# A 7-tap convolution and a gated feed-forward block: the order of the opening's weights, loads and late passes

## The chip, the cores and the metric

One core of a Trainium2 chip runs the whole program. The metric is the device time of one execution in microseconds (us); the median of several runs stands for a kernel.

The engines in this text: PE is the matrix engine (TensorE) and PEld its weight loads, DVE is VectorE, ACT is ScalarE, POOL is GpSimd, SP is SyncE, which here only issues DMAs and waits. Each engine takes its instructions in the order in which the program gives them; semaphores carry the waits between engines.

## The reference

Input x has 8 sequences of 4096 tokens with 192 channels. Each of 8 heads has 24 channels and 7 taps; the taps are the softmax of the head's row of `weight`.

```python
w = softmax(weight)                        # 8 heads x 7 taps
y[b, s, h, :] = sum_k w[h, k] * x_pad[b, s + k, h, :]   # causal: six zero rows ahead
g = y @ w_gate                             # 192 -> 1536
v = y @ w_val
out = (g * sigmoid(g) * v) @ w_out         # 1536 -> 192
```

All inputs and the output are float32; the matrix products run in float16 with float32 sums.

## The kernel before, in words

**Blocks and chunks.** The 32768 tokens go in blocks of 512; two blocks are a pair. The 1536 hidden channels go in 12 chunks of 128. For each block and chunk, PE makes gate and val (L563 and L564, three passes of 64 rows each side by side in the two halves of the array), ACT makes silu of the gate (L568), DVE multiplies by val into `h` (L570). The second product (`acc`, L575) takes the `h` of the block before, a few pieces behind each chunk. Chunks are counted through the program: block 0 has chunks 0 to 11, block 1 has 12 to 23, pair 1 begins at 24. Gate has 2 PSUM buffers, val 3; the bank `run` is a single one, which also serves the gate of chunk 2; `acc` has one buffer of two banks.

**Convolution, normally.** From pair 1 on, each pair's x comes as squares of 32 by 32 (`sqA` for channels 0 to 127, `sqB` for the last 64 channels of both blocks; `emit_load`, L103) that DVE transposes (`emit_turn`, L114) into channels by tokens. Then three groups (0 is A's first block, 1 is B, 2 is A's second block) run the taps by channel with weights `wn`: ACT starts `run` (L490) and makes products (L483), DVE adds others onto `run` (L500), POOL makes two or three products and adds everything (L505, L512), joins the result `xc` (L518), and SP copies it with its halves swapped (`xs`, L466 and L467). SP has a wait of its own (`mark`, L460) on PE in each block.

**The opening.** Pair 0 (blocks 0 and 1) has its convolution done by PE instead, with a band matrix `T` and x as it lies in memory, because that starts earlier. Block 0: x lands in `x_sb`, is cast into `x16` by ACT and POOL, `heads` multiplies it by `T`, ACT and DVE fold the sums, `gather` sorts them by channel through `spread` into `D0`, `D1`, `D2`. `spread` is filled by four POOL copies, `place(0)` to `place(3)`. Block 1 comes later, while block 0's chunks are running: its x (`load_x(1, ...)`) is cast by POOL into `x16p` (L240, after everything else that POOL does at the start), and three late passes of `convolve` by `halves` (L366, into `acc`) follow chunks by the list `todo`: `lateA(0)`, `lateA(1)` with `outA` (ACT folds into `foldA1`, SP swaps it into `swapA1` by L674) and `lateC` (`foldC1`, `swapC1`). Chunk 12 takes the folds in its first half passes and the swaps in its second ones. In the trace these tiles stand as foldA, swapA, foldC, swapC.

**Channel taps.** `spread_taps` (L443, L444) makes `wn` for the groups: two small matmuls of `parts` (the taps in three float16 pieces, made by POOL), and a sum by DVE. Before, it stands in PE's order between the first passes of chunks 0 and 1 and their second ones.

**Order.** The schedule is by hand: instructions go to each engine as the program lists them. `at_chunk(c, f)` puts work behind chunk c (its gate, silu and h first). The plan's `opening` gives pair 1's three groups chunk numbers in the form (turn, start, ACT taps, DVE taps, POOL taps, join, swap). `loadA` issues pair 1's squares A behind the transpose of its squares B. The weights of gate and val come in three parts of four chunks (`load_w`, issued by POOL, L169), and w_out behind `x16p` (L615).

Of the kernel before, what the change touches and what calls it, by code (L numbers as in the profile page):

```python
# [14 lines left out]
    swap=(10, 11, 13),  # L15
    load=((2, -47), (3, -40), (0, -34), (1, -28)),
    opening=(
        (11, 13, (14, 15), (14, 15), 12, 16, 20),
        (2, 3, (5, 9), (4, 8), 3, 10, 13),
        (18, 20, (22, 23), (21,), 20, 23, 31),  # L20
    ),
    gate=2, val=3, lead=4, third=(2,),
# [4 lines left out]
def kernel(  # L27
# [9 lines left out]
    nc = tc.nc  # L37
    fp32 = mybir.dt.float32
# [10 lines left out]
    P = 128  # L49
# [3 lines left out]
    TB = P * SUBS  # L53
    NCH = Dff // P
# [21 lines left out]
    squares, xts = {}, {}  # L76
# [5 lines left out]
    def emit_load(q, part, half=None):  # L82
        head = q % ppb == 0
        if part == 2 and not half:
            squares[q, "A"] = headA if head else xpool.tile(
                [P, HIST + 2 * TB], fp32, tag="sqA", name="sqA"
            )
            squares[q, "B"] = headB if head else xpool.tile(
                [P, HIST + TB], fp32, tag="sqB", name="sqB"
            )  # L90
        for k in range(2):
            quad = 2 * (part % 2) + k
            if part < 2:
                tile_, t0, n, c = squares[q, "A"], 0, 2 * TB, SQ * quad
            else:
                tile_, t0, n, c = squares[q, "B"], TB * (part % 2), TB, P + SQ * k
            skip = HIST if head and t0 == 0 else 0
            row = q * 2 * TB + t0 - HIST + skip
            n = n // SQ + 1 - skip // SQ
            if half is not None:  # L100
                first = TB // SQ + 1
                skip, row, n = ((skip, row, first), (first * SQ, row + first * SQ, n - first))[half]
            nc.sync.dma_start(  # L103
                out=tile_[quad * SQ : (quad + 1) * SQ, skip : skip + n * SQ].rearrange("p (n c) -> p n c", c=SQ),
                in_=x_flat[row : row + n * SQ, c : c + SQ].rearrange("(n p) c -> p n c", p=SQ),
            )
# [9 lines left out]
    def sync_after(ins, earlier, why="one bank, two halves of the array"):  # L116
        tc.add_manual_dep(
            ins.ins,
            earlier.ins.name,
            mybir.DependencyInfo(mybir.DependencyClass.Sync, mybir.DependencyReason.DATA),  # L120
            reason=why,
        )
# [4 lines left out]
    HALF, STEP, W, NW = TB // 2, 85, 96, 6  # L127
# [20 lines left out]
    def load_x(b, lo, hi, queue=nc.sync):  # L148
        queue.dma_start(
            out=x_sb[0:LOADED, b, lo:hi, :],  # L150
            in_=bass.AP(
                tensor=x_flat.tensor,
                offset=x_flat.offset + (b * TB + starts[b][lo]) * D,
                ap=[[D, LOADED], [STEP * D, hi - lo], [1, D]],
            ),
        )
# [10 lines left out]
    def load_w(lo, hi, which):  # L167
        rows, src = w_halves[which]
        nc.gpsimd.dma_start(out=w[rows, :, lo * P : hi * P], in_=src[:, :, lo * P : hi * P])  # L169
# [52 lines left out]
    nc.vector.memset(spread, 0.0)  # L222

    mask = const_pool.tile([RT, D], fp16, tag="mask", name="mask")
    load_w(0, 4, 0)
    load_w(0, 4, 1)


    x16 = xpool.tile([P, NW, D + 8], fp16, tag="x16", name="x16", bufs=1)
# [47 lines left out]
    def repeated(t):  # L277
        return t[:, :].unsqueeze(1).to_broadcast([RT, REP, 8])
# [4 lines left out]
    left_second = nc.vector.scalar_tensor_tensor(  # L283
        out=left[0:RT, 1, :, :], in0=repeated(turned), scalar=norm, in1=left[0:RT, 0, :, :],
        op0=ALU.mult, op1=ALU.subtract,
    )
    left = left[:, :, :, :].rearrange("r i n m -> r i (n m)")

    sync_after(nc.sync.nop(), left_second, "squares behind the first weights")
    if n_pairs > 1:  # L290
        for part in (2, 3):
            emit_load(1, part, None)
    load_x(1, 0, 3)
    load_x(1, 3, NW)
    nc.scalar.activation(two, one, AF.Silu)
    cast(nc.scalar.copy, 0, 3)
    sync_after(cast(nc.gpsimd.tensor_copy, 3, NW), left_second, "not beside the taps")
# [1 line left out]
    def place(k):  # L299
        lo, hi, at = ((0, DB, 0), (DB, 96, 0), (0, 32, 32), (32, 96, 0))[k]  # L300
        nc.gpsimd.tensor_copy(
            spread[:, k, :, at : at + hi - lo], plain[:, lo:hi].unsqueeze(1).to_broadcast([P, 2, hi - lo])
        )

    place(0)
    place(1)
    nc.gpsimd.memset(mask, 0.0)
    nc.gpsimd.affine_select(
        out=mask[:, :].rearrange("r (h c) -> r h c", h=H),
# [1 line left out]
        pattern=[[-8, H], [0, grp]],  # L311
        compare_op=ALU.not_equal, fill=1.0, base=0, channel_multiplier=1,
    )
    load_w(4, 8, 0)
    load_w(4, 8, 1)
    place(2)
    place(3)
    own = const_pool.tile([RT, P], fp16, tag="own", name="own")
    nc.gpsimd.tensor_copy(
        own[:, :].rearrange("h (t c) -> h t c", t=2),  # L320
# [7 lines left out]
    nc.gpsimd.tensor_tensor(rest, raw, parts[:, 0, :], op=ALU.subtract)  # L328
    nc.gpsimd.tensor_copy(parts[:, 1, :], rest)
    nc.gpsimd.tensor_tensor(parts[:, 2, :], rest, parts[:, 1, :], op=ALU.subtract)  # L330
    for b in range(2):
        load_w(8, NCH, b)

# [20 lines left out]
    def convolve(banks, quarters, parts, parities):  # L356


        fresh = set()
        for part in parts:  # L360
            for e in parities:
                for n in range(len(quarters[0])):
                    for a, q in enumerate(quarters):
                        x, h, u0, out = q[n](e)
                        k = len(banks) * out.start // TB
                        ins = nc.tensor.matmul(  # L366
                            banks[k][32 * a : 32 * a + 32, out], x,
                            T[0:ROWS, part, h, u0 : u0 + out.stop - out.start],
                            start=part + e == 0 and (a, k) not in fresh,
                            stop=part == 1 and e == parities[-1], skip_group_check=True,  # L370
                        )
                        fresh.add((a, k))
        return ins
# [10 lines left out]
    def by_block(b, half):  # L384
        def of(e, w):
            h = 32 * b // grp
            h += (h + e) % 2
            return x16p[0:ROWS, e, w, 32 * b : 32 * b + 32], h, *piece(1, w, HALF * half)

        return [lambda e, w=w: of(e, w) for w in range(half * NW // 2, (half + 1) * NW // 2)]  # L390
# [49 lines left out]
    def spread_taps(bank):  # L440
        ps = bank[:, 0 : 6 * K].rearrange("p (g t k) -> p g t k", g=2, k=K)
        for g, which in enumerate((mask[:, 0:P], own)):
            nc.tensor.matmul(ps[:, g, :, :], which, parts, start=True, stop=True)  # L443
        nc.vector.tensor_reduce(wn, ps.rearrange("p g t k -> p g k t"), axis=AX.X, op=ALU.add)  # L444
# [180 lines left out]
    tpool = ctx.enter_context(tc.tile_pool(name="run", bufs=1, reuse_waits="tile", space=bass.MemoryType.PSUM))  # L625
# [6 lines left out]
    def at_chunk(c, f):  # L632
        todo.setdefault(c, []).append(f)
# [27 lines left out]
    def late_sum():  # L661
        late["sum"] = apool.tile([P, 2, 512], fp32, tag="acc", name="acc")

    def halves(g, bank):
        return convolve([bank], [by_block(2 * g + a % 2, a // 2) for a in range(4)], (0, 1), (0, 1))

    def lateA(g):
        if g == 0:
            late_sum()
        halves(g, late["sum"][:, g, :])  # L670

    def exchange(out, fold):
# [18 lines left out]
        at_chunk(2 * NCH, blank)  # L691

    late = {}
    at_chunk(5, lambda: lateA(0))
    at_chunk(6, lambda: lateA(1))
    at_chunk(6, outA)
    at_chunk(8, lateC)

    def loadA(half):
        if not half:  # L700
# [4 lines left out]
    if n_pairs > 1:  # L705
        for g, plan in enumerate(PLAN["opening"]):
            plan_group(1, g, *plan)
        for half, c in enumerate((2, 16)):
            at_chunk(c, lambda half=half: loadA(half))
    for q in range(2, n_pairs):  # L710
        base = 2 * NCH * q
        for part, c in PLAN["load"]:
            c = {2: 20, 3: 20, 0: 26, 1: 27}[part] if q == 2 else base + c
            at_chunk(c, lambda q=q, part=part: emit_load(q, part))
        for g in range(3):
            c = base + PLAN["start"][g]
# [13 lines left out]
    for n in range(2 * n_pairs):  # L730
        block = Block(n)
        for j in range(NCH):
            src, units = before if j < NCH - lead // 4 else block, late_start.get(at, 4)
            if n == 0:
                src, units = block, 0
            elif n == 2 * n_pairs - 1 and src is block:
                units = 0
            los, his = src.second(units)
            half = src.done // (2 * NCH) - 1 if units and src.done % (2 * NCH) == 0 else None
            if n == 0 and j < 2:  # L740
                if j == 0:
                    block.first(0, (0,))
                    block.first(1, (0,))
                    spread_taps(tpool.tile([P, TB], fp32, tag="run", name="run"))
                block.first(j, (1, 2))
            elif half is None:
                block.first(j)
            for lo, hi in zip(los, his):
                lo()
                hi()  # L750
            if half is not None:
                src.evacuate(half)
                block.first(j)
            block.gate(j)
            if half is not None:
                src.store(half)
            for f in todo.pop(at, ()):
                f()
            at += 1
        before = block  # L760
# [61 lines left out]
```

## Time and profile before

| what | value |
|---|---|
| median of 3 runs | 773.06 us (772.67 to 773.37) |
| the profiled execution | 773.51 us, of which span 771.7 us |
| PE busy | 763.0 us, 99% of the span |
| POOL, ACT, DVE busy | 668.7, 661.5, 658.4 us |
| granted clock of PE | 1.000 |
| block 1's x: issue, and landing of its second half | 6.76 and 7.30; 14.86 us |
| chunks 4 to 7's weights: issues | 6.36 and 7.01 us |
| swapA: issue and landing | 18.76; 23.50 us |

The profile comes from one execution; its times count from the span's start. Some 1.8 us of an execution lie outside the span. In the windows a row has the stretch, its length, then the busy time of PE, PEld, DVE, ACT and POOL with counts of instructions, the granted clock, the DMA engines' share and GB/s. In the chain of waits a row has start, length and what the time went to; "SPq" is an issue by SP, "DMA a<-b" a transfer. Queue q0 carries POOL's transfers, q1 SP's.

### The profile page before, as it was taken

The page shows a single profiled execution, that of the slowest core. Times are in us where ns is not written, and L with a number is a line of the kernel's source. Part 1 is how long each engine was busy: PE and PEld are TensorE (multiplying, and loading weights), DVE is VectorE, ACT ScalarE, POOL GpSimd, SP SyncE. Part 2 cuts the span into 40 slices and gives each one's busy share as a digit, 9 for nine tenths or more (in the row PEclk, how much of TensorE's full clock was granted, in tenths as well). Part 3 has the DMA queues.
Part 4 walks back from the last instruction along what each step waited for, and adds up shares of the span by engine and source line. Part 5 has one row for each costly group of instructions (what it writes and reads, how often), then busy time and mean ns, then how long its engine had stood idle before and what let it go on. Part 6 is the DMA issues. An engine that isn't in the chain of part 4 may idle for free.

```text
span 771.7 us, 28287 instructions
## 1 busy us (share of the span) xinstructions
PE 763.0 (99%) x11036; PEld 596.0 (77%) x11036; DVE 658.4 (85%) x1046; ACT 661.5 (86%) x1188; POOL 668.7 (87%) x654
## 2 busy tenths in 40 slices
PE   7999999999999999999999999999999999999998
PEld 3767777777777777777777777777777777778997
DVE  6788888889888888888888888888888888888875
ACT  6788888888888888888888888888888888888875
POOL 6898988888988889988889888899888899888850
PEclk9999999999999999999999999999999999999999
DMA  8553344433444343444334434334343433443211
GB/s 143 101 109 83 83 95 85 93 87 79 88 88 93 85 85 87 87 88 96 83 80 86 94 84 95 86 83 87 82 99 82 89 85 87 89 89 90 62 46 54
DMA packets 255287, 67.28 MB, mean 87 GB/s; under 512 B 207920, under 2 KB 255152, under 8 KB 255152
## 3 DMA queue, kind: packets, MB, share of 16 engines
q1 hardware_dynamic: 252048, 63.48, 37.6%
q0 software_dynamic: 2800, 1.77, 1.7%
q8 instruction: 86, 1.41, 0.8%
q14 instruction: 49, 0.40, 0.2%
q10 hardware_dynamic: 304, 0.22, 0.1%
HBM read 29.65 MB, written 25.17 MB: 71 GB/s over the span
## 4 chain that ended last, share of the span: by engine, by line
PE 96%; DMA 2%; SPq 1%; DVE 0%; ACT 0%; issue 0%; POOL 0%; DVEq 0%
PE val L564 48%; PE acc L575 34%; PE gate L563 13%; DMA x_sb<-in_x_dram 1%; DMA swapA<-foldA 1%; SPq L103 0%; DMA sqB<-in_x_dram 0%; PE acc L773 0%; PE idle L257 0%; POOL x16p L240 0%; PE val L773 0%; PE run L773 0%; DVE h L570 0%; ACT foldA L677 0%; SPq L467 0%
## 5 line engine op out<-in xcount | busy, mean ns | idle before, releaser
L570 DVE TENSOR_TENSOR h<-silu,val 128x512 f16<-128x512 f16 x768 | 508.9, 680 | 102.2 <-ACT silu L568 70.3
L568 ACT ACTIVATE silu<-gate 128x512 f16<-128x512 f32 x768 | 453.1, 594 | 81.2 <-PE gate L563 72.7
L575 PE MATMUL acc<-wo_sb,h 64*128 64x192 f16 x6048 | 465.6, 243 | 1.1 <-DVE h L570 1.1
L512 POOL TENSOR_TENSOR t<-t,t 128x512 f32<-128x512 f32 x310 | 393.9, 1271 | 61.1 <-ACT t L483 37.9
L575 PEld LDWEIGHTS <-h 64*128 64x128 f16 x6048 | 394.9, 94 | 60.8 <-DVE h L570 1.4
L563 PE MATMUL gate<-xc,w_sb 64*128 64x512 f16 x1116 | 409.8, 376 | 0.0
L564 PE MATMUL val<-xc,w_sb 64*128 64x512 f16 x1116 | 409.7, 376 | 0.0
L563 PE MATMUL gate<-xs,w_sb 64*128 64x512 f16 x1116 | 360.1, 376 | 0.0
L564 PE MATMUL val<-xs,w_sb 64*128 64x512 f16 x1116 | 360.0, 376 | 0.0
L564 PEld LDWEIGHTS <-w_sb 64*128 64x128 f16 x2340 | 211.8, 94 | 96.8 <-issue 1.8
L563 PEld LDWEIGHTS <-w_sb 64*128 64x128 f16 x2340 | 212.0, 94 | 5.0 <-issue 1.5
L518 POOL TENSOR_TENSOR xc<-t,aD 128x512 f16<-128x512 f32 x93 | 118.1, 1270 | 7.3
L505 POOL TENSOR_SCALAR t<-xtA,wn 128x512 f32<-128x512 f32 x155 | 106.1, 696 | 0.7 <-DVE xtA L114 0.7
L483 ACT ACTIVATE t<-xtA,wn 128x512 f32<-128x512 f32 x124 | 88.6, 714 | 0.0
L613 ACT COPY o<-acc 128x384 f32<-128x384 f32 x126 | 60.4, 479 | 18.7 <-PE acc L575 5.4
L500 DVE SCALAR_TENSOR_TENSOR aD<-xtA,wn,run 128x512 f32<-128x512 f32 x62 | 45.9, 740 | 0.0
L483 ACT ACTIVATE t<-xtB,wn 128x512 f32<-128x512 f32 x62 | 44.3, 714 | 0.0
L490 ACT ACTIVATE run<-xtA,wn 128x512 f32<-128x512 f32 x62 | 42.5, 686 | 0.6 <-DVE xtA L114 0.6
L505 POOL TENSOR_SCALAR t<-xtB,wn 128x512 f32<-128x512 f32 x62 | 42.3, 697 | 0.0
L114 DVE STREAM_TRANSPOSE xtA<-sqA 128x544 f32<-128x544 f32 (+1 forms) x48 | 34.6, 721 | 1.0 <-DMA sqA<-in_x_dram 1.0
L500 DVE SCALAR_TENSOR_TENSOR run<-xtB,wn,run 128x512 f32<-128x512 f32 x31 | 23.2, 749 | 0.0
L500 DVE SCALAR_TENSOR_TENSOR run<-xtA,wn,run 128x512 f32<-128x512 f32 x31 | 23.2, 749 | 0.0
(112 smaller groups left out, 178.9 us busy)
## 6 DMA issues: line engine op xcount, KB each, us to landing
out_dram<-o SPq DMA_DIRECT2D x127, 192.0 KB, 2.0
sqA<-in_x_dram SPq DMA_DIRECT2D x92, 132.0 KB, 3.1
xs<-xc SPq DMA_DIRECT2D x186, 64.0 KB, 2.0
sqB<-in_x_dram SPq DMA_DIRECT2D x96, 68.0 KB, 2.3
headA<-in_x_dram SPq DMA_DIRECT2D x28, 128.0 KB, 2.7
headB<-in_x_dram SPq DMA_DIRECT2D x14, 68.0 KB, 2.5
headB<-in_x_dram SPq DMA_DIRECT2D x14, 64.0 KB, 2.1
x_sb<-in_x_dram SPq DMA_DIRECT2D x3, 216.0 KB, 5.0
```

What stands on the lines that cost most here:

```text
L483: mul(parts[-1], *self.tap(k))
L490: nc.scalar.mul(self.aD, *self.tap(0))
L500: nc.vector.scalar_tensor_tensor(out=self.aD, in0=v, scalar=s, in1=run, op0=ALU.mult, op1=ALU.add)
L505: self.product(k, lambda t, v, s: nc.gpsimd.tensor_scalar(t, v, scalar1=s, scalar2=1.0, op0=ALU.mult, op1=ALU.mult), self.parts)
L512: nc.gpsimd.tensor_tensor(self.parts[0], self.parts[0], t, op=ALU.add)
L518: nc.gpsimd.tensor_tensor(xc, self.parts[0], self.aD, op=ALU.add)
L563: nc.tensor.matmul(g, w[0:DB, ca, f], a[0:DB, :], start=(i == 0), stop=(i == 2))
L564: nc.tensor.matmul(v, w[DB:P, cb, f], b[DB:P, :], start=(i == 0), stop=(i == 2))
L568: nc.scalar.activation(s, self.g.pop(j), AF.Silu)
L570: nc.vector.tensor_tensor(h, s, self.v.pop(j), op=ALU.mult)
L575: ins = nc.tensor.matmul(acc, self.h[j][r, ts(s, P)], wo_r[r, j, :], start=first and j == 0, stop=not first and j == NCH - 1, skip_group_c ...
L613: nc.scalar.copy(self.o[:, 2 * half : 2 * half + 2, :], self.acc[:, :, 0:D])
```

## The change

Five things are moved; the arithmetic stays.

- POOL issues the weights of chunks 4 to 7 directly behind those of chunks 0 to 3, and those of chunks 8 to 11 behind the four `place` copies; mask, `own` and `parts` come after these issues.
- SP issues block 1's x ahead of pair 1's squares B.
- `spread_taps` runs behind chunk 1, in the second bank of `acc`.
- The late passes run behind chunks 4, 5 and 7, where they ran behind 5, 6 and 8.
- In the plan of pair 1, group 0 has its transpose at chunk 12 (11 before) and POOL's taps at 13 (12). Group 1 has its transpose at 3 (2), its start and POOL taps at 4 (3), ACT taps at 6 and 9 (5 and 9), DVE taps at 5 and 8 (4 and 8). The first half of squares A is issued at chunk 3 (2).

```diff
     opening=(
-        (11, 13, (14, 15), (14, 15), 12, 16, 20),
-        (2, 3, (5, 9), (4, 8), 3, 10, 13),
+        (12, 13, (14, 15), (14, 15), 13, 16, 20),
+        (3, 4, (6, 9), (5, 8), 4, 10, 13),
         (18, 20, (22, 23), (21,), 20, 23, 31),
...
-    load_w(0, 4, 0)
-    load_w(0, 4, 1)
+    for lo in (0, 4):
+        for b in range(2):
+            load_w(lo, lo + 4, b)
...
-    sync_after(nc.sync.nop(), left_second, "squares behind the first weights")
+    sync_after(nc.sync.nop(), left_second, "block 1's x behind the first weights")
+    load_x(1, 0, 3)
+    load_x(1, 3, NW)
     if n_pairs > 1:
         for part in (2, 3):
             emit_load(1, part, None)
-    load_x(1, 0, 3)
-    load_x(1, 3, NW)
...
     place(0)
     place(1)
+    place(2)
+    place(3)
+    for b in range(2):
+        load_w(8, NCH, b)
     nc.gpsimd.memset(mask, 0.0)
...
-    load_w(4, 8, 0)
-    load_w(4, 8, 1)
-    place(2)
-    place(3)
...
-    for b in range(2):
-        load_w(8, NCH, b)
...
+    def late_taps():
+        late_sum()
+        spread_taps(late["sum"][:, 1, :])
+
     def lateA(g):
-        if g == 0:
-            late_sum()
         halves(g, late["sum"][:, g, :])
...
-    at_chunk(5, lambda: lateA(0))
-    at_chunk(6, lambda: lateA(1))
-    at_chunk(6, outA)
-    at_chunk(8, lateC)
+    at_chunk(1, late_taps)
+    at_chunk(4, lambda: lateA(0))
+    at_chunk(5, lambda: lateA(1))
+    at_chunk(5, outA)
+    at_chunk(7, lateC)
...
-        for half, c in enumerate((2, 16)):
+        for half, c in enumerate((3, 16)):
             at_chunk(c, lambda half=half: loadA(half))
...
                     block.first(1, (0,))
-                    spread_taps(tpool.tile([P, TB], fp32, tag="run", name="run"))
                 block.first(j, (1, 2))
```

## The prediction

> **What bounds the kernel now.** I read the page's chain of waits first, then busy time by stage, then the chain in order of time.
>
> ```profile
> PE 96%; DMA 2%; SPq 1%; DVE 0%; ACT 0%; issue 0%; POOL 0%; DVEq 0%
> ```
>
> TensorE carries 96% of the span, and nothing in its steady work changes. So a gain can only be TensorE idle time of the opening. Stages (length, then busy time of PE, PEld, DVE, ACT, POOL):
>
> ```profile
> 14.00:17.50 3.50, 1.70 (x63) 0.81 (x65) 1.96 (x4) 1.85 (x4) 2.56 (x4) 1.00 0.57 90
> 22.00:24.00 2.00, 1.30 (x15) 0.64 (x12) 1.59 (x4) 1.05 (x3) 1.71 (x2) 1.00 0.33 80
> 24.00:37.00 13.00, 13.00 (x257) 12.39 (x256) 10.27 (x16) 10.97 (x20) 11.77 (x12) 1.00 0.43 88
> 37.00:39.00 2.00, 0.86 (x16) 0.43 (x12) 1.50 (x3) 1.43 (x4) 1.84 (x3) 1.00 0.20 62
> ```
>
> The second column is PE: full from 24 to 37, with holes before 24 and another near 38. The chain (start, length, what) names both. First hole:
>
> ```profile
> 7.30 7.56 DMA x_sb<-in_x_dram
> 14.91 1.28 POOL x16p L240 x2
> ...
> 18.15 0.59 ACT foldA L677
> 18.76 4.74 DMA swapA<-foldA
> 23.54 0.27 PE gate L563
> ```
>
> Block 1's x lands at 14.86, is cast, convolved late, folded, swapped by DMA, and block 1's first chunk (chunk 12) can only use the swap at 23.54. Second hole:
>
> ```profile
> 32.10 0.47 SPq L466
> ...
> 34.98 2.40 DMA sqB<-in_x_dram
> ...
> 38.17 0.66 DVE h L570
> 38.88 0.26 PE acc L575 x2
> ```
>
> SP issues A0's swap (group A, first half, of pair 1) at 32.10, behind it the squares B of pair 2; they land at 37.38, and VectorE stands at their transpose. So I work out one instant, T, when chunk 12 takes its swapped operands (23.54 before), and then what the second hole does.
>
> **Front, to chunk 4.** GpSimd's issues of chunks 4 to 7 (0.65 + 0.63) move from 6.36 to 3.58. It idled from 3.58 to 4.68, so its x cast starts at 2.09 + 0.85 + 0.64 + 0.65 + 0.63 = 4.86, call it 4.88: 0.20 late. The heads' second half is not touched: it waited until 6.37 for T anyway. foldA and D0 come 0.2 late (D0 ends 8.28). The spreads 2 and 3 no longer stand behind DMA issues, so the last gathers start at 7.70 (foldC's 7.61 plus a hop) and not 7.93; D1 is cast by 8.82, D2 by 8.94. The taps no longer stand in front of chunk 0's second pass, which waited until 9.62 for `parts`; it starts at 8.90. Gain so far 0.72.
>
> The taps now come after chunk 1, at 9.77 on PE. GpSimd's parts: cast 4.88, 0.61 to the spreads, four at 0.20, issues 1.27, mask 0.67, own 0.26, parts 1.25: 9.75. So PE loses about 0.1. Their bank is D1's, read out by 8.82, and the second late pass, which takes it next, comes long after the reduce. The reduce of wn (0.20) now sits between h1 and h2 on VectorE; chunks 3 and 4 wait for val buffers from h0 and h1, ahead of it. Chunk 3 starts at 10.90 (11.65 before). Chunk 4 waited for weights until 12.66; with them issued 2.8 earlier it starts at 11.55, and h3 ends at 12.85. The issues now run beside VectorE's tap operations (3.40 to 4.61), where before GpSimd stood still; no row shows the two together. I take nothing: the issues took 0.63 to 0.66 wherever they stood. If they cost the taps 0.3 of their 1.2 us, that is hidden up to the 0.95 found below.
>
> **Transfers.** Service goes in bursts. Per stretch (queue: packets, MB, share), 9.5 to 10.25, 10.5 to 11.25, and 17.5 to 21.5:
>
> ```profile
> q1 hardware_dynamic: 242, 0.18, 79.9%
> q0 software_dynamic: 54, 0.04, 35.5%
> ```
>
> ```profile
> q0 software_dynamic: 115, 0.12, 93.6%
> q1 hardware_dynamic: 62, 0.04, 25.9%
> ```
>
> ```profile
> q0 software_dynamic: 1312, 0.50, 117.1%
> ```
>
> x and weights take turns by whole transfers, and swapA, issued at 18.76, moves nothing before 21.5, while w_out's 576 KB run. The engines are full from 6 to 14, so times add up. From 6.25, where chunks 0 to 3's weights end: weights of 4 to 7 2.0 (384 KB at the 190 GB/s of the stretch 12.5 to 14), x 1.7 (432 KB, bursts at 240 GB/s or a little over), squares B 1.6 (272 KB; 119 GB/s while SP was issuing them, 200 to 217 in the best slices), weights of 8 to 11 2.0. x's data end at 9.5 to 10.2. Landing comes later than the bulk: 0.4 for squares B, 2.3 for x's second half. So x lands between 10.3 and 12.2; I take 11.4.
>
> The Trainium skill, page "DMA: Bandwidth & Descriptors", section "Queues, rings and completion order", says that each engine alternates between queue rows after at most 64 descriptors; the 17.5 to 21.5 row does not show that for swapA. By that rule swapA would land about 1.5 sooner and the sum would be set by ScalarE (below), with nothing else moved.
>
> **Block 1's x and the late passes.** The passes are the same, one chunk earlier each. The casts follow landing, the first late pass ends 1.84 after it (14.86 to 16.70 before): 13.24, and chunk 5 follows. This is covered as long as x lands by 12.8, since another wait is later:
>
> **Squares B behind x.** They now issue at 5.65 to 7.73, behind x, among the weights of 8 to 11. In order of arrival their data end at 6.25 + 2.0 + 1.7 + 1.6 + 1.0 = 12.55, taking turns at 13.55; with a landing lag of 0.4 to 2.0 the ends are 12.9 and 15.6. I take 13.8: the means of the two orders (13.05) and a lag nearer to the squares' own row. The transpose is placed one chunk later, yet VectorE reaches it at 12.85. So it stands for about 0.95 us, with h4 behind it, and ScalarE's `run` behind the transpose:
>
> ```profile
> 12.71 0.73 DVE L114 STREAM_TRANSPOSE xtB<-sqB 128x544 f32<-128x544 f32 x1
> ...
> 13.54 0.69 ACT L490 ACTIVATE run<-xtB,wn 128x512 f32<-128x512 f32 x1 [0.65 <-DVE xtB L114]
> ```
>
> `run` starts 0.83 after the transpose and holds ScalarE 0.63; silu 5 therefore starts at 13.8 + 0.05 + 0.83 + 0.63 = 15.3. From there ScalarE is continuous: silu 5 0.50, foldA 0.58, silu 6 0.49, tap 0.61, silu 7 0.50, foldC 0.36, silu 8 and 9 0.99, tap 0.61, silu 10 0.59, in all 5.23. Chunk 12 needs silu 10's gate buffer: 20.6 with a hop, and its swap pass follows 0.35 later: T = 20.95. TensorE's own passes fit below it.
>
> **The swap.** loadA's four DMAs follow the transpose on SP (1.92), so swapA issues at 16.6 and 17.2, foldA ending at 16.4. It has 3.8 us to land after the second issue; 4.5 was the case beside w_out, 1.9 to 2.6 for other swaps. w_out is issued at 12.7, not 16.13, so its data end near 18.6, plus 0 to 1.5 for the squares A now beside it; swapA lands 1.5 after (23.5 against 22.0): 20.1 to 21.6. SwapC issues from 18.4 and needs until about 21.2, its place 0.33 behind T. I keep T = 20.95: 2.6 earlier than 23.54.
>
> **The second hole.** A0's transpose moves from chunk 11 to 12: behind h12, which waits for T. Counted in before's times, h12 ends at 25.45, the transpose at 26.15, and GpSimd's group A0, which began at 24.80, begins there: 1.35 later relative to TensorE. Its work is continuous, 6.76 (24.80 to 31.56), so xc ends at 32.91 and SP's swap goes from 32.10 to 32.95. Squares B of pair 2, the transpose and h23 follow: the second hole grows by 0.85. SP had 0.5 us of slack there; it is used up. The 0.3 us that ScalarE's later `run` takes from chunk 16 vanishes in the same hole.
>
> **Sum:** 2.6 - 0.85 = 1.75 us. The profiled execution was 773.51 (771.7 span plus 1.8 around it) and becomes 771.75; against the median 773.06, 771.3. A measurement here can tell about 0.2%, 1.55 us.
>
> **Rivals.**
> - *Squares land with the third weights' middle* (14.1 to 15.5): everything from the transpose slips one for one, T is 21.25 to 22.65, the gain 0 to 1.5: 771.6 to 773.1, no change by the bound. For it: x's second half landed 2.3 after its bulk. Against it: squares landed 0.4 after theirs. 0.38.
> - *Slower: squares land only after the last weights.* Decides at 23.54 - 0.85 = 22.69 for T, so at a landing of 15.55; the last weights' DMA needed 6.0 from its issue at 10.15, and behind a backlog of 7.3 us, not 5.5, a lag of 2.7 puts the squares at 16.3: T = 23.45, 0.75 lost, 773.8; slower by over 1.55 needs 17.1. The same section of the Trainium skill says that a completion signal lands only after every earlier write of that engine, on all its queues; x's second half agrees (6 packets of its queue after 12.5, landing at 14.86), no row here shows it for squares. 0.12, of which 0.07 lies over the bound, with the mishaps not named here.
> - *Everything covered:* squares land by 12.85; silu 5 starts at 14.3, T = 20.0, gain 2.7: 770.4. If A0's group also finds its slack, 769.5. 0.1.
> - *The reorder does nothing for x*: it lands with the weights at 14 or later. Then chunk 5 is 1.2 later than ScalarE's path and T about 22.1; 772.5. The 9.5 to 10.25 row speaks against it. 0.02, counted within 0.2%.
>
> **How the numbers follow.** The forecast case (landing 13 to 14.1) has 0.38, with 770.5 to 771.6; 771.3 is its time. Faster by over 0.2% is this and the covered case, 0.48; within 0.2% the first and the last rival and the milder half of the slower one, 0.45; slower 0.07. The range 770.3 to 773.5 leaves out about 0.05 below and 0.12 above; it takes in the ends 12.9 and 15.6 of the squares' landing.
>
> **What would show it.** Right: the chain of the opening no longer holds x_sb; chunk 0's second pass at 8.9; chunk 4 without a weights wait; the wait list has the transpose of xtB on squares B, near 1 us; chunk 12's swap pass near 21; the wait on squares B of pair 2 longer than 1.3 us, h23 about 1.75 earlier. Wrong: VectorE passes the first transpose without a wait; x16p still first in PE's waits; swapA landing past 22; or SP's swap of A0 still held by TensorE rather than by GpSimd.

## The result, and the profile after

The changed kernel takes 774.93 us (median of 16 runs, 773.18 to 776.99); the kernel before took 773.07 us beside it (16 runs). The ratio is 1.0022, 95% interval 1.0012 to 1.0033: slower; the interval reaches from under to over the 0.2% that a measurement here can tell. The forecast was 771.3, range 770.3 to 773.5. The profiled execution took 775.58 us, its span is 773.8 (before: 773.51 and 771.7).

**The share of the chain and the stages.** The chain of the profile's page, then busy time by stage (start and end, length, PE, PEld, DVE, ACT, POOL, granted clock, DMA share, GB/s):

```profile
PE 95%; DMA 1%; SPq 1%; POOL 1%; issue 1%; DVE 1%; ACT 0%; DVEq 0%; POOLq 0%; ACTq 0%
```

```profile
14.00:17.50 3.50, 2.90 (x108) 1.56 (x109) 1.32 (x2) 0.69 (x2) 2.24 (x3) 1.00 0.55 62
22.00:24.00 2.00, 1.36 (x12) 0.50 (x8) 2.00 (x4) 1.16 (x3) 1.59 (x2) 1.00 0.38 76
24.00:37.00 13.00, 12.34 (x243) 11.85 (x244) 9.91 (x17) 9.73 (x18) 10.38 (x11) 1.00 0.34 70
37.00:39.00 2.00, 1.97 (x28) 1.10 (x22) 0.47 (x1) 1.94 (x4) 1.84 (x3) 1.00 0.86 178
37.00:41.00 4.00, 1.97 (x28) 1.10 (x22) 1.80 (x4) 2.49 (x5) 3.76 (x4) 1.00 0.49 106
```

PE (third number) gained 1.2 us between 14 and 17.5, because block 1's x comes earlier. It lost 0.66 between 24 and 37, where it was full before, and stands still from 39 to 41.

**The first hole.** The chain in order of time (start, length, what):

```profile
9.28 6.67 DMA sqB<-in_x_dram
15.95 0.02 issue
15.97 0.76 DVE xtB L114
...
16.81 0.69 ACT run L489
17.50 0.52 ACT silu L567
...
22.56 0.60 ACT silu L567
23.17 0.18 SPq L675
23.34 0.04 issue
23.39 1.87 DMA swapC<-foldC
...
25.30 0.28 PE val L563
```

The late x is gone from the chain, as forecast. In its place stand pair 1's squares B (landed 15.95), behind them VectorE's transpose, ScalarE's `run` and its row of silus, and at the end swapC, landed at 25.26. On PE, chunk 12's first pass, its first pass with swapped operands (the forecast's T) and its first one with the last swap are:

```profile
22.72 0.27 PE L562 MATMUL gate<-foldA,w_sb 64*128 64x256 f16 x1 [0.27 <-ACT silu L567]
...
23.62 0.27 PE L562 MATMUL gate<-swapA,w_sb 64*128 64x256 f16 x1 [0.25 <-DMA swapA<-foldA]
...
25.30 0.27 PE L563 MATMUL val<-swapC,w_sb 64*128 64x256 f16 x1 [0.38 <-DMA swapC<-foldC]
```

ScalarE's silu of chunk 10 lets chunk 12 begin at 22.72, where the forecast had 20.6. T is 23.62: forecast 20.95, before 23.54. The passes behind T then wait once more for swapA (24.21) and for swapC (25.30). The wait list from 12 to 42 us (engine, line, releaser: total, times, longest):

```profile
DVE xtB L114 <- DMA sqB<-in_x_dram: 5.1, 2, 2.9
ACT run L489 <- DVE xtB L114: 5.0, 2, 3.5
POOL x16p L241 <- DMA x_sb<-in_x_dram: 3.5, 1, 3.5
```

Before, the same list has for this wait only the one on pair 2's squares B:

```profile
DVE xtB L114 <- DMA sqB<-in_x_dram: 1.3, 1, 1.3
```

The forecast had about 1 us in the first row's longest wait; it is 2.9, and the same row holds the wait on pair 2's squares B, 2.2 (5.1 less 2.9).

**The second hole,** from the same chain:

```profile
26.31 0.76 DVE xtA L114
...
27.15 1.37 POOL t L504 x2
...
32.63 1.28 POOL xc L517
33.93 0.47 SPq L465
...
36.81 2.73 DMA sqB<-in_x_dram
...
40.34 0.66 DVE h L569
```

A0's transpose stands behind h of chunk 12 (25.68 to 26.3), GpSimd's A0 directly behind it, SP's swap directly behind GpSimd (33.93), and pair 2's squares B land at 39.54. h23 starts at 40.34, 2.17 later than before.

**Two numbers hold the whole difference.** h of chunk 12 starts at 25.68 instead of 24.80: 0.88 later, where the forecast had 22.2 (T of 20.95, and 1.26 from T to h12 as before). From there to the span's end it is 748.1 instead of 746.9: 1.2 more, forecast 0.85. Together 2.1, the difference of the spans. I call them *h12* and *the distance*, and read each experiment by them. But h12 moves from one execution to the next: e7 below, whose program is the same up to there, has 24.38 in its profile, 1.3 earlier. One profile's h12 shows no difference smaller than that.

### The profile page after: what moved, and what is told of

It reads as the page before. It is cut to its first block, busy times and chain, and to the rows that moved or that the text cites. A ratio compares the mean times of both kernels' runs of the same rounds, so it can differ in the third digit from the quotient of the medians.

```text
span 773.8 us, 28288 instructions
## 1 busy us (share of the span) xinstructions
PE 763.7 (99%) x11036; PEld 525.3 (68%) x11036; DVE 658.0 (85%) x1046; ACT 658.2 (85%) x1188; POOL 667.8 (86%) x654
## 4 chain that ended last, share of the span: by engine, by line
PE 95%; DMA 1%; SPq 1%; POOL 1%; issue 1%; DVE 1%; ACT 0%; DVEq 0%; POOLq 0%; ACTq 0%
PE gate L562 56%; PE acc L574 32%; PE val L563 6%; DMA sqB<-in_x_dram 1%; SPq L103 1%; POOL t L511 0%; PE acc L774 0%; DMA swapC<-foldC 0%; PE idle L258 0%; ACT silu L567 0%; DVE h L569 0%; POOL t L504 0%; POOL xc L517 0%; PE val L774 0%; PE run L774 0%
## 5 line engine op out<-in xcount | busy, mean ns | idle before, releaser
L574 PEld LDWEIGHTS <-h 64*128 64x128 f16 x6048 | 290.1, 94 | 127.6 <-DVE h L569 2.3
L574 PE MATMUL acc<-wo_sb,h 64*128 64x192 f16 x6048 | 363.1, 243 | 2.1 <-DVE h L569 2.1
L489 ACT ACTIVATE run<-xtB,wn 128x512 f32<-128x512 f32 x31 | 21.3, 687 | 5.0 <-DVE xtB L114 5.0
```

The lines of the kernel that those rows point to most:

```text
L489: nc.scalar.mul(self.aD, *self.tap(0))
L574: ins = nc.tensor.matmul(acc, self.h[j][r, ts(s, P)], wo_r[r, j, :], start=first and j == 0, stop=not first and j == NCH - 1, skip_group_c ...
```

## The experiments

Line numbers in the edits' text are the changed kernel's. Times are medians; the ratio is to the kernel before on the same chip, with its 95% interval.

### Where did the squares stay? The order of the weights, the order on SP

`e1_squares_first`: SP's order of before, all else changed.

```diff
-    load_x(1, 0, 3); load_x(1, 3, NW)
     for part in (2, 3):
         emit_load(1, part, None)
+    load_x(1, 0, 3); load_x(1, 3, NW)
```

> The changed kernel with SP's order of before: squares B ahead of block 1's x. Theory SQUARES (the loss is VectorE and ScalarE standing at the first transpose until squares B land at 15.95, because they are queued behind x on SP): squares land near 9 to 10, the transpose runs near 12.9 without a wait, block 1's x lands at 14 to 15, chunk 12 takes its swaps near 23, and the time is 772.5 to 773.5. Theory WEIGHTS (the loss is that chunks 4 to 7's weights, issued early, keep the engines from everything else): squares still land after 12.9 and x after 15, and the time stays at 774.5 to 775.5.

Measured 777.71, ratio 1.0060 (1.0047 to 1.0073). Issued first, at 4.64, the squares still landed only at 15.1. From their issues to landing, here and before, where they were issued at the same time:

```profile
DMA to landing us min/median/max: 7.1/7.9/8.4
```

```profile
DMA to landing us min/median/max: 2.7/2.8/2.9
```

So it is not x ahead of them that holds them. Both signs of WEIGHTS came (squares after 12.9, x after 15), but the time is 2.2 us over its range, because of something no theory had: x landed at 16.16, PE had nothing to do, and the granted clock (third number from the right) was cut.

```profile
14.00:16.00 2.00, 0.00 (x0) 0.00 (x0) 0.88 (x2) 0.04 (x1) 0.00 (x0) 0.71 0.18 47
16.00:18.00 2.00, 0.86 (x40) 0.67 (x44) 0.44 (x1) 0.66 (x1) 1.78 (x3) 0.50 0.40 63
18.00:20.00 2.00, 2.00 (x50) 0.77 (x42) 0.00 (x0) 0.19 (x1) 1.88 (x3) 0.50 0.87 98
```

`e2_weights_back`: GpSimd's order of before, x still ahead of the squares.

```diff
-    for lo in (0, 4): ...               # weights of chunks 0 to 7 first
+    load_w(0, 4, 0); load_w(0, 4, 1)    # 4 to 7 behind the mask, 8 to 11 behind parts
```

> The changed kernel with GpSimd's order of before (chunks 4 to 7's weights at 6.4, chunks 8 to 11's behind the taps' parts); x stays ahead of squares B. Theory WEIGHTS: x lands near 8.5 to 9.5, squares B near 11 to 12, ahead of the transpose; chunk 4 waits for its weights until about 13; chunk 12 takes its swaps near 21.5, and the time is 771 to 772.5. Theory SQUARES (behind x is what counts): squares still land near 14 or later, and the time is 774 to 775.

Measured 773.43, ratio 1.0006 (0.9997 to 1.0014): no loss against the kernel before can be told. This lies between the two theories: the time is 0.9 us over the range of WEIGHTS and 0.6 under that of SQUARES, squares B landed at 13.97, as SQUARES had it, and VectorE still waited 0.9 for them; h12 came at 23.77. The DMA queues between 6 and 8 us (queue: packets, MB, share of the 16 engines; q0 carries GpSimd's weights, q1 SP's x and squares) show what differs. Before:

```profile
q1 hardware_dynamic: 2062, 0.26, 82.6%
q0 software_dynamic: 54, 0.04, 17.6%
```

The changed kernel:

```profile
q0 software_dynamic: 189, 0.17, 78.2%
q1 hardware_dynamic: 9, 0.01, 1.4%
```

With the weights back:

```profile
q1 hardware_dynamic: 950, 0.46, 91.0%
q0 software_dynamic: 50, 0.04, 12.5%
```

With chunks 4 to 7's weights queued at 3.58, SP's queue moved 9 packets in these two microseconds, although x had been issued at 4.64; the two queues together moved 0.18 MB, where it is 0.30 before and 0.50 in e2. The 16 engines were busy for only 80% of this time, so whether x stood there for want of an engine, or because its own descriptors came late, the trace does not show. Nor does any run separate the two parts that e2 puts back: chunks 8 to 11's weights too were early in the changed kernel (issued at 6.24, before at 9.50). The picture repeats: in the ten profiles with the weights early and x first (the changed kernel and nine variants below), q1 moved 9 to 74 packets between 6 and 8, q0 0.17 to 0.27 MB; in the five with the weights back, q1 moved 950 to 1115 packets. Squares B landed at 15.6 to 17.0 wherever the first group shows it, at 13.6 to 14.7 in the second. SP itself is held as well. The DMA issues of SP (start, length, what), changed kernel:

```profile
4.64 0.82 SPq L149 DMA_DIRECT2D x_sb<-in_x_dram  x2
5.50 6.03 SPq L103 DMA_DIRECT2D sqB<-in_x_dram  x4
16.81 2.70 SPq L103 DMA_DIRECT2D sqA<-in_x_dram  x4
19.61 3.10 SPq L675 DMA_DIRECT2D swapA<-foldA  x2
```

Four issues of squares B took 6.03 us; in e2 they took 2.73, before 2.08:

```profile
4.64 2.08 SPq L103 DMA_DIRECT2D sqB<-in_x_dram  x4
```

### The front alone

`e4_taps_only`: the kernel before with the channel taps behind chunk 1.

```diff
+    at_chunk(1, late_taps)
...
-                    spread_taps(tpool.tile([P, TB], fp32, tag="run", name="run"))
```

> The kernel before with one part of the change: the channel taps behind chunk 1, in the accumulator's second bank. Chunk 0's second pass starts near 9.2 and not at 9.62, but the first late pass still waits for block 1's x at 14.9. All theories: no change, 772.8 to 773.4; if the reduce between h1 and h2 cost something, it would be 773.3 to 773.8.

Measured 772.78, ratio 1.0003 (0.9994 to 1.0013), no change, as expected. Chunk 0's second pass starts at 9.11 (9.62 before), so the front does gain. h12 came at 24.06 and not at 24.80, but because x landed at 14.1 in this profile and at 14.86 in the one before; that transfer is not part of the edit, and what the front gains does not reach the time.

### The second hole

`e5_group0_back`: the changed kernel with group A0's plan of before.

```diff
-        (12, 13, (14, 15), (14, 15), 13, 16, 20),
+        (11, 13, (14, 15), (14, 15), 12, 16, 20),
```

> The changed kernel with group 0's plan of before: A0's transpose at chunk 11 and GpSimd's taps at 12. Theory SECOND HOLE (0.85 us of the loss comes from A0's transpose standing behind h12, which starts GpSimd's group A0 late and SP's swap and pair 2's squares B after it): GpSimd starts A0 right behind its join of B near 24.9 and not at 27.15, SP's swap of A0 is again released by TensorE near 33.2, and the time falls by 0.7 to 0.9, to about 774.1. Rival (the second hole has another cause, the first hole alone made the loss): no change, 774.6 to 775.2.

Measured 774.26, ratio 1.0017 (1.0008 to 1.0026). GpSimd starts A0 at 24.75, right behind group B, SP's swap goes at 31.91, the wait on pair 2's squares B falls from 2.2 to 1.3, and the distance from 748.1 to 747.25. With the transpose at chunk 12 it is 747.8 to 748.05 in e1, e2, e3, e7, f1 and f2; with the plan of before it is 746.6 to 746.9 in the kernel before, e4, f4 and g4. The remaining profiles with it at chunk 12 lose more behind h12 for other reasons (squares A in e6, the clock in e8, group B in f3, w_out in g1 and h1). So the trace bears the second-hole step out; the time is as expected, but its interval overlaps that of the changed kernel, so that it shows no fall by itself.

`e7_pair2_squares_early`: the changed kernel with pair 2's squares B issued behind chunk 17 (20 before), so that they do not follow A0's swap on SP.

```diff
-            c = {2: 20, 3: 20, 0: 26, 1: 27}[part] if q == 2 else base + c
+            c = {2: 17, 3: 17, 0: 26, 1: 27}[part] if q == 2 else base + c
```

> The changed kernel with pair 2's squares B issued behind chunk 17 and not behind chunk 20, so that on SP they stand ahead of A0's swap. Theory SECOND HOLE: VectorE no longer waits for them at 37.5 (2.2 us in the changed kernel's trace), TensorE's hole near 39 closes, and the time falls by about 2, to 772.7 to 773.1. Rival (the hole follows GpSimd's lag, and something else of pair 1's groups stops the chain as late): a fall of under 0.7, to 774.2 or more.

Measured 774.89, ratio 1.0020 (1.0009 to 1.0030): nothing gained. The wait of VectorE on these squares is gone, and with it PE's hole at 36 to 40, but in the stretch from 28 to 48 VectorE now waits for squares A of group A2, and PE for SP's `mark`, which queues behind the squares' issues:

```profile
DVE xtA L114 <- DMA sqA<-in_x_dram: 1.6, 1, 1.6
...
PE acc L574 <- SPq L459: 1.1, 1, 1.1
```

### VectorE's stand, and the swaps behind it

`f1_group1_late`: group B three chunks later, so that nobody stands for squares B.

```diff
-        (3, 4, (6, 9), (5, 8), 4, 10, 13),
+        (6, 7, (9, 11), (8, 10), 7, 11, 13),
...
-        for half, c in enumerate((3, 16)):
+        for half, c in enumerate((6, 16)):
```

> The changed kernel with group B of pair 1 moved back by three chunks: its transpose behind chunk 6, start and GpSimd taps behind 7, ScalarE taps 9 and 11, VectorE taps 8 and 10, join 11, squares A behind chunk 6. STANDING theory (what was lost is the 2.93 us that VectorE stood for squares B, and ScalarE behind it): squares B have landed when VectorE comes to them, no wait over 0.3 there, ScalarE has no 3.48 us wait, h12 of chunk 12 starts near 22.0 instead of 25.68, and with 747.9 to 748.1 from there the span is 770.0 and the time 771.8 (771.3 to 772.6). SWAPS rival (the standing only covered the transfers of the swaps behind w_out): no wait at the squares, but swapA and swapC still land at 23.5 or later and h12 starts at 24.0 or later: 773.8 or more. CLOCK rival: TensorE's hole before the late passes (x lands at 13.25) is followed by a granted clock under 0.9 and the time is 775 or more.

Measured 774.55, ratio 1.0016 (1.0004 to 1.0028). VectorE no longer waits at the first transpose, and h12 came at 24.75, 0.9 earlier than in the changed kernel's profile, but not earlier than in those of e5 and e7 (24.45, 24.38), where VectorE stands as in the changed kernel. The swaps rival holds: SP now issues squares A from 18.80 to 21.57 and swapC behind them, and PE waits for swapC until 23.8. What the stand costs by itself is not shown: without it, the swap is as late.

`e3_squaresA_late`: squares A behind the swaps on SP (`enumerate((8, 16))`). `e6_weights_back_squaresA_late`: the same on top of e2.

> The changed kernel with the first half of squares A issued behind chunk 8 and not behind chunk 3, so that SP issues both swaps ahead of it. Theory SWAPS (chunk 12 took its swaps at 25.3 because SP was still issuing squares A and their queue stood behind w_out): swapA is issued at 18.5, swapC at 20.4, they land by 22.5, chunk 12 takes them near 23, and the time is 772.5 to 773.3. Theory SQUARES (ScalarE's chain behind the late transpose sets chunk 12 at 22.7 and the rest is small): 774 to 774.7.

> e2 (GpSimd's order of before, x ahead of squares B) with the first half of squares A behind chunk 8. Theory SWAPS (once x is early, chunk 12 waits only for swaps that stand behind squares A, which stand behind w_out on SP's queue): swapA is issued near 16.7 and lands by 20, chunk 12 takes its swaps near 21.3 (about 23 in e2), and the time is 771.2 to 772. Rival (squares A come too late for A0's transpose, and VectorE stands there): the first hole closes but the second grows by as much, 773 to 774.

e3: 777.33, ratio 1.0052 (1.0039 to 1.0065). The swaps were in time, but squares B landed at 16.7 in this profile, ScalarE stood 4.4 us, PE waited 1.8 for it, and then ran at half clock:

```profile
18.00:20.00 2.00, 1.17 (x30) 0.58 (x33) 1.24 (x3) 2.00 (x5) 1.92 (x3) 0.87 1.49 181
20.00:22.00 2.00, 2.00 (x48) 1.04 (x38) 1.45 (x3) 1.12 (x3) 1.58 (x2) 0.50 0.43 78
```

e6: 775.01, ratio 1.0023 (1.0012 to 1.0034). SwapC was issued at 18.38 instead of 20.9, but squares A landed only at 24.86, A0's transpose waited 1.79 for them and GpSimd 2.7 behind it. The rival's mechanism holds, though the time is 1 us over its range: the swap's gain is paid by the squares moved behind it.

`f2_w_out_split`: w_out in two DMAs, the second half issued behind chunk 8. `g1_w_out_half_behind_11`: behind chunk 11. `h1_w_out_half_behind_h9`: when h of chunk 9 is done.

```diff
-    nc.gpsimd.dma_start(out=wo_r, in_=...)
+    load_wo(0, NCH // 2)
...
+    at_chunk(8, lambda: load_wo(NCH // 2, NCH))    # f2; 11 in g1; a wait on h9 in h1
```

> The changed kernel with w_out in two DMAs, the second half issued behind chunk 8. SWAPS theory (squares A and the swaps stand in line behind w_out's data): swapA's second issue is no longer held until 22.7, swapC lands by 23.5 instead of 25.26, ScalarE's silu 10 then sets chunk 12, h12 starts near 24.0 instead of 25.68: span 772.0, time 773.8 (773.3 to 774.3). STANDING rival: ScalarE's path, late by the squares' landing, sets chunk 12 anyway; h12 moves by less than 0.5, time 774.5 to 775.

> The changed kernel with w_out in two DMAs, the second half issued behind chunk 11 (in f2_w_out_split it was issued at 19.38, 0.3 us ahead of the swaps' first issue at 19.71). SWAPS theory (the swaps wait for whatever data were queued before them): with only 288 KB of w_out, issued near 13.7, and squares A in front, swapA lands by 22.5, swapC by 23.3, and h12 starts near 23.8 (ScalarE's path) instead of 25.68: span 771.9, time 773.7 (773.2 to 774.3). Rival: squares A alone, or the swaps' own two issues, hold them; swapC lands past 24.5 as in f2, h12 after 25.0, time 774.8 or more.

> The changed kernel with w_out in two DMAs; GpSimd issues the second half only when h of chunk 9 is done (near 22.2), behind the swaps' issues and some 5 us ahead of the place where g1's TensorE stood for it (27). SWAPS theory: as in g1 both swaps land about 2 us after their issue, h12 starts near 24.9 (25.68 before the edit), no wait on w_out over 0.5: span 772.9, time 774.1 to 774.8. Rival: the half lands after 27.5, TensorE stands for it and time is 775.5 or more.

f2: 775.62, ratio 1.0028 (1.0018 to 1.0038). The half was issued at 19.38, just ahead of swapA (19.71), and swapA took 3.5 to 4.3 us to land: no gain, h12 at 25.79. g1: 777.88, ratio 1.0062 (1.0050 to 1.0074). With the half behind them the swaps land in 1.8 to 2.0 us. SwapA, then swapC, from issue to landing:

```profile
DMA to landing us min/median/max: 1.9/2.0/2.0
```

```profile
DMA to landing us min/median/max: 1.8/1.8/1.9
```

SwapA took 2.1 to 4.0 us in the changed kernel and 3.5 to 4.3 in f2, and here SP's second issue of it was not held either. So the swaps do wait for the data of w_out queued ahead of them. h12 came at 24.95, 0.73 earlier than in the changed kernel's profile, but later than in e7's with w_out whole, so that this difference is no price. And the half, issued at 25.48, is needed from 27 on. PE stands for it:

```profile
PE acc L574 <- DMA wo_sb<-in_moe_w_out_dram: 3.2, 1, 3.2
```

h1: 777.14, ratio 1.0043 (1.0030 to 1.0055). The swaps land in 1.8 to 2.0 again, the half goes out only at 24.21, where 22.2 was expected, because squares B landed at 17.0 in this profile, and PE stands 1.9 us for it. Here the rivals hold: of the three places tried for the half, one is ahead of the swaps and two are too late.

`f3_group1_late_w_out_split` joins f1 and f2. `f4_before_w_out_split` and `g4_before_w_out_half_behind_8` are e4 with w_out split, the half behind chunk 4 or 8.

> Both edits together. If each cost lies on its own path and the later one sets chunk 12, both removed give h12 near 21.8, span 769.9, time 771.7 (771.0 to 772.4), and less than either alone by at least 0.5. If the rivals hold (granted clock cut after the hole at 13 to 14, or squares A late for A0's transpose, whose landing then sets group A0), 774 or more.

> The kernel before with the channel taps behind chunk 1 and w_out in two DMAs, the second half issued behind chunk 4. The late x stays (landing near 14). SWAPS theory: swapA lands near 21 instead of 22.7, h12 starts 1 us or so earlier than with the taps alone (24.06), span 769.9, time 771.7 (771.2 to 772.3). Rival: the second half of w_out is now the one that stands in front of the swaps, or is late for block 0's second product behind chunk 15; no gain, 772.8 or more.

> The kernel before with the channel taps behind chunk 1 and w_out in two DMAs, the second half issued behind chunk 8, where GpSimd waits 0.9 us anyway (in f4 it was issued at 18.92, ahead of the swaps at 19.33). SWAPS theory: swapA (issue 17.98) lands near 21 instead of 22.74, h12 starts near 23.0 instead of 24.06: span 769.9, time 771.7 (771.2 to 772.3). Rival: the second half runs into swapC (issue 19.74), or TensorE's hole at 14 to 16 is followed by a cut clock as in f4 (0.50 from 16 to 18): 773.5 or more.

f3: 774.37, ratio 1.0022 (1.0010 to 1.0034); h12 at 23.05, 2.6 earlier than in the changed kernel's profile and 1.3 earlier than in e7's, but the distance is 748.5: group B ends later on GpSimd, and A0 starts only behind it, at 25.47. f4: 774.08, ratio 1.0019 (1.0007 to 1.0030), swapA landed at 23.9, since its data now follow the second half, issued at 18.92. g4: 774.35, ratio 1.0022 (1.0012 to 1.0032), where I expected that half behind the swaps; GpSimd reached it at 19.3, ahead of swapA at 19.76. All three miss the times forecast, f4 and g4 because the half still lay ahead.

### The clock

`e8_filled_hole`: five products of zeros behind chunk 4 of the changed kernel, into a bank not yet in use, so that PE stands less there.

> The changed kernel with five matmuls of zeros behind chunk 4, into the accumulator's bank that the first late pass then overwrites; they stand where TensorE waited from 12.8 to 14.0. Theory CLOCK (part of the loss, and the spread of the changed kernel's times from 773.2 to 777.0, is the clock being cut in runs in which TensorE's holes before chunk 12 grow long; the mean clock of its runs was between 0.996 and 1.0): the clock stays at 1.000 in nearly all runs, the median falls to 774.2 to 774.7 and the spread shrinks to 1.5 us. Rival (the spread comes from the DMA engines alone): clock and spread stay, and the time is 774.7 to 775.5.

Measured 777.69, ratio 1.0059 (1.0047 to 1.0071). In its profile swapC landed at 26.34, PE was idle from 24 to 26, and the clock was cut behind that hole, 0.50 from 26 to 32. Theory CLOCK failed: it had the clock at 1.000 in nearly all runs, and all five have a mean of 0.995 to 0.998. The rival failed too, which had the time at 775.5 at most. Why swapC took 3.8 us there, with the engines nearly idle, stays open.

### Both losses taken back

`g2_weights_back_group0_back`: e2 and e5 together. What is left of the change is x ahead of the squares, the taps behind chunk 1, the late passes one chunk earlier and group B's plan. `g3_g2_w_out_half_behind_11` and `h2_g2_w_out_half_behind_h9` add the split of w_out.

> The changed kernel with GpSimd's order of the kernel before (as in e2_weights_back, h12 at 23.77) and with group A0's transpose back at chunk 11, its GpSimd taps at 12. If the two losses add (weights' order: h12 from 25.68 to 23.77; A0's place: 748 to 747 from h12 to the end), h12 near 23.8, the wait on pair 2's squares B 1.3 instead of 1.95, span 770.8, time 772.6 (772.0 to 773.2). Rival: A0's squares (issued 14.82 to 16.84, behind w_out) or group B's late end hold group A0 anyway: 773.3 or more.

> The kernel of g2 with w_out in two DMAs, the second half issued behind chunk 11. SWAPS theory: swapA (issue 16.93, its second DMA held until 20.8 in e2) lands by 21.5 and swapC by 22, h12 starts near 22.7, 1 us earlier than in g2: span 769.8, time 771.6 (771.0 to 772.3), which would beat the kernel before. Rival: ScalarE's or VectorE's own path sets chunk 12 near 23.4, or the second hole takes the gain back as squares B of pair 2 follow GpSimd's A0, not chunk 12: 772.6.

> The kernel of g2 (GpSimd's order of before, group A0 back at chunk 11) with the same second half of w_out behind h of chunk 9. SWAPS theory: swapA's second issue is no longer held, swapC lands by 22.5, h12 starts near 22.7, 747.0 from there: span 769.7, time 771.5 (771.0 to 772.4), which beats the kernel before. Rival: the half is late for TensorE, or group A0 and with it pair 2's squares B keep their time, so that the second hole takes the gain back: 772.6 or more.

g2: 772.61 beside 773.25 for the kernel before, the expected time to the digit, but the ratio is 0.9999 (0.9984 to 1.0014): no difference that can be told. Its runs spread from 771.78 to 777.49. In the six whose mean granted clock was 1.000 the median is 772.01 (kernel before in the same session: 773.09, 17 runs); in the other six, 774.88. The profiled one belongs to the latter (span 774.1, swapA's second issue held 3.05 us on SP, swapC landed at 25.0), so it does not show how the others gained. With both losses taken back none is left to be told. That the second adds to the first does not follow from the times: e2 alone has 1.0006 (0.9997 to 1.0014).

g3: 778.88, ratio 1.0073 (1.0052 to 1.0094), with PE standing 3.5 us for the half of w_out and half clock from 30 to 36. h2: 774.41, ratio 1.0018 (1.0007 to 1.0029). It has the earliest h12 of all, 22.76, as expected, and then pays for it:

```profile
PE acc L575 <- DMA wo_sb<-in_moe_w_out_dram: 2.6, 1, 2.6
```

No kernel here beats the kernel before by more than the measurement can tell.

## Why the prediction was wrong, point by point

**The front: nearly right, to chunk 3.** Chunk 0's second pass starts at 9.09 (forecast 8.90, before 9.62), chunk 3 at 11.09 (10.90, before 11.65). Chunk 4 was to start at 11.55 with no wait for weights; it starts at 12.09 and waits for val's, which landed 7.9 us after their issue. Of 2.8 us of earlier issue, 0.6 arrived.

**The transfers: the step that failed.** "The engines are full from 6 to 14, so times add up" was summed at 190 GB/s for the weights. At that rate 6 to 8 us would have taken 0.38 MB; they moved 0.17 (0.27 at most in the ten profiles), and next to nothing moved beside them. I had taken the row of 9.5 to 10.25, where both queues move, for the rule; in the two microseconds just behind the first weights the queue that had been filled earlier moves nearly alone: q0 in the changed kernel, q1 before and in e2. This is why the squares had landed so fast before. x landed at 13.25 (forecast 11.4, range 10.3 to 12.2; 11.8 to 13.25 in the ten profiles), squares B at 15.95 (13.8, range 12.9 to 15.6; 15.6 to 17.0). The lag from data to landing was not the error: the last packets of the squares moved between 15.25 and 15.5, where the sum had the end of their data at 12.55 to 13.55. That e2 has them at 13.97, near the forecast, bears nothing out, since there the weights are not moved.

The Trainium skill, page "DMA: Bandwidth & Descriptors", section "Queues, rings and completion order", has each DMA engine go round its queue rows, a packet at a time. Here 9 packets of q1 stand against 189 of q0 although x had been issued at 4.64, so this stretch does not bear that out, unless q1's descriptors were late.

**From the transpose on: the mechanism right.** Squares B came 2.15 later than forecast, and silu 5 started at 17.50 instead of 15.3, 2.2 later. ScalarE's row from there to silu 10 took 5.2, as forecast, and chunk 12 began at 22.72 instead of 20.6.

**The swaps: wrong by the same step.** Forecast 20.1 to 21.6 for swapA, 21.2 for swapC. But w_out is issued behind x's cast, at 14.49 and not at 12.7, SP could issue squares A only from 16.81, swapA from 19.61, its second DMA was held until 22.7 with w_out's data (16 to 20.5) and squares A's (20 to 22) ahead, and swapC landed at 25.26. So of the 3.5 us between the forecast h12 (22.2) and the measured one (25.68), 2.1 are chunk 12's late beginning, which is the squares' landing. The swaps account for the rest, 1.35: T comes 0.90 behind the beginning where I had 0.35, and h12 2.06 behind T where I had 1.26. This holds for the one profile; in e7's, which begins chunk 12 at 22.33, the rest is 0.4, and neither is a price of the swaps in the time.

**The second hole: right, a little too small.** Forecast 0.85, measured 1.2 against the kernel before and 0.9 against e5, in their profiles.

**The rivals.** The case that came true is *squares land only after the last weights*, with its point at 15.55, given 0.12 (the last weights, issued by 7.5, landed near 15.2). Its own working at a landing of 15.95 gives T = 23.1, a profiled execution of 773.9 and no change by the bound; the measured 775.58 has 1.3 more at chunk 12, from the swaps, and 0.35 more in the second hole. I gave it a small chance because squares had landed 0.4 after their bulk in the trace of before; but that row was measured with no weights of chunks 4 to 7 queued ahead of them, and it was the bulk that came late. The rival's own reason, a longer lag, did not come true.

**What no step had: the clock.** Of the changed kernel's 16 runs, 9 had a mean granted clock under 1.000 (median 775.58, against 774.79 for the 7 others); of the 118 runs of the kernel before in the sessions of the experiments, 23. The runs at full clock alone are still 1.7 us over the median 773.07 (full-clock medians of the kernel before in the experiments: 772.8 to 773.3), so the clock adds to the loss and is not its cause.

## What to carry to other kernels

Here, weights queued earlier on one queue moved back what another had to deliver in that stretch (the squares' landing went from 2.7 to 2.9 us behind their issue to 7.1 to 8.4 in e1): read, in the same window, how many packets each queue moved, before adding up transfer times. In this opening, weights, squares, swaps and w_out could each be hurried only at another's cost in the places tried, so the price of the one that becomes late belongs in the sum. A step that is moved one place behind an event that itself waits takes over that event's lateness.

## What the runs showed of the hardware

- **Short holes can go with a halved clock.** In g4 PE stood only once for over 0.3 us between 8 and 20, from 12.51 to 14.20. Busy time by stage:

```profile
12.00:14.00 2.00, 0.50 (x2) 0.09 (x1) 1.79 (x3) 1.24 (x2) 0.00 (x0) 1.00 1.16 194
14.00:16.00 2.00, 1.80 (x10) 0.70 (x11) 0.10 (x1) 0.60 (x2) 1.50 (x3) 0.52 0.67 106
```

  The granted clock fell to 0.52 directly behind a hole of 1.7 us. The kernel before has a hole of 1.5 us (14.13 to 15.62) and kept 1.00 in its profile; the changed kernel and g1 have holes of 1.1 and 1.2 us at 13 to 14, and g1 was cut from 16 to 19 where the changed kernel was not. And one program, the kernel before, had a cut clock in 23 of 118 runs. So the length of the hole alone does not decide it; it differs from run to run. The Trainium skill, page "TensorE: Matmul & The Clock Gate", Part 1, has the gate close after an idle window of about 3.4 us that runs freely. The difference between runs fits a free-running window, the length does not: in g4 the cut came behind 1.7 us.
- **An issue can take several times as long.** SP's four issues of squares B took 2.08 us before and 6.03 after, and its second issue of swapA 2.5 (0.6 before). What stands behind such an issue on SP waits too. What holds it, the trace does not name.
- **The landing varies.** With the same order of weights and x, squares B landed between 15.6 and 17.0 and x between 11.8 and 13.25 in the ten profiles, and h12 came at 25.68 in the changed kernel and at 24.38 in e7, with the same program up to there. Differences of about 1 us in one profile's opening prove little.
